# A first matrix product in 21 half-size products a step for 22, with one crossed tile of the convolution

## The chip, the cores and the metric

The kernel runs on one core of one Trainium2 chip. The metric is the device time in microseconds of one execution. The kernel before takes 2438.4 us, the median of three runs (2438.39 to 2438.45). The execution that the profile shows took 2438.89 us.

## The reference

The input `x` holds 8 sequences of 4096 tokens with 192 channels, in float32. A causal convolution of seven taps runs along the tokens; the taps are the softmax of an 8 x 7 weight, one row for each group of 24 channels. The result goes through a two-layer network with a gelu in between:

```python
w = softmax(weight, axis=-1)                       # 8 heads x 7 taps
y[b, s, c] = sum(w[c // 24, k] * x_pad[b, s + k, c] for k in range(7))
h = y.reshape(32768, 192) @ w_in                   # 192 x 2048
g = h / (1 + exp(-1.702 * h))
out = g @ w_out                                    # 2048 x 192
```

`w_in` and `w_out` arrive in float64 and are rounded to float32 inside the kernel. All matrix products are in float32.

## The kernel before

The work goes in 64 steps of 512 tokens (two halves of T = 256 tokens from two halves of the batch). Two neighbouring steps, an even and an odd one, share one "big" block of convolved input, so there are 32 big blocks.

A step has two matrix products on TensorE. The first, `product1` (L374 to L386), multiplies a block of `w_in` (64 channels by 256 columns) with a block of the convolved input (64 channels by 256 tokens). A call issues four matmuls, each of which the profile shows as two records; the two row halves of the array work at the same time on different columns of `w_in`. The second, `product2` and `quarters` (L470 to L500), multiplies 32-column pieces of `w_out` with the gelu's output `g`, four pieces at a time in the four column groups of the array.

Both products use sums of blocks to need fewer block products, in the manner of Strassen and Winograd. The first product has two units of work a step, one for each half of the columns of `w_in`. A unit is a product of 2 by 3 by 2 blocks (column halves, channel blocks of 64, token halves), which takes 12 block products plainly and 11 here, so a step has 22. The class `Unit` (L388 to L468) names them: `p1` to `p7` write into the PSUM tiles `slots` and `sums`, `seed` copies a partial product from a slot to `sums`, `keep2` and `keep3` copy intermediate results out, `add22` and `add12` add them on VectorE, and `h11` to `h22` apply the gelu on ScalarE. `sum_g` (L464) forms the four sums of `g` that the second product needs. Step 0 uses the plain form, 24 block products.

The convolved input is in the tile `f`. Its 128 partitions hold the 64 channels of the even step's tokens in the lower half and those of the odd step's tokens in the upper half. As both row halves of the array need the tokens of the step in hand, a copy of each half in the other half is made by `cross` (L351), two DMAs on SP's queue (SyncE). In the kernel before, `f` has room for both: index 0 of its second axis is the original and index 1 the crossed copy, and the pool holds two such tiles.

The order of instructions on each engine is the order in which they are written (`manual_schedule`). The preparation of the next big block is a list of pieces, `prepare` (L360 to L372): transposes of `x`, the load of the block after it, 21 convolution operations, four sums of `f` (`sums_c`) and the crossing. `work(n)` takes the next n pieces and issues them at that place. In an odd step one call `work(None)` (L732), in the middle of the first product, takes all that is left. `output` (L532 to L572) holds the second product, the final adds and transposes (`Out.turn`), and the six stores (`Out.store`, on SP's queue).

Within `output`, the last product p7 is followed on VectorE by two adds, a transpose, a subtraction and a transpose (L567 to L571), and the stores wait for these transposes. The main loop (L698 to L766) ends with `output`, and the next step's first `product1` follows it directly on TensorE.

Of the kernel before, what the change touches and what calls it, by code (L numbers as in the profile page):

```python
# [15 lines left out]
def kernel(  # L16
# [7 lines left out]
):  # L24

# [24 lines left out]
    P = 128  # L50
# [28 lines left out]
    hu_pool = ctx.enter_context(tc.tile_pool(name="hu", bufs=2))  # L79
# [42 lines left out]
    NB = 9  # L122
    C11, C12, C21, C22, C31, C32, V1, V2, V4 = range(NB)
    V3 = C12


    NA = 10
    W11, W12, W13, W21, W22, W23, X1, X2, X4, X5 = range(NA)
    X3 = W21
    w_in_s = consts.tile([P, NU, NA, UW], F32)  # L130
# [14 lines left out]
    assert PIECE == CW * D and NW * 2 * PIECE == 3 * NK * T and 6 * PIECE == 2 * NB * T  # L145
    raw = g[:, T1 : T4 + 1, :, :].rearrange("p s f t -> p (s f t)").bitcast(U32)
    raw = raw.rearrange("p (i n) -> p i n", i=NW)
    diag = consts.tile([P, NC, K, P], F32)
    assert min(NC * K * P, 2 * NJ * XW) >= 3 * PIECE

    def scratch(flat):
        return [flat[:, j * PIECE : (j + 1) * PIECE].bitcast(U32) for j in range(3)]

    tmp = f_pool.tile([P, 2, NB, T], F32, name="f").rearrange("p o b t -> p (o b t)")
    sets = [
        scratch(tmp),
        scratch(tmp[:, 3 * PIECE :]),
        None,
        scratch(diag.rearrange("p c k q -> p (c k q)")),
# [87 lines left out]
    def round_w_in(i):  # L247
        u, m = divmod(i, 2)
        dst = w_in_s[:, u, NC * m : NC * (m + 1), :]
        round_piece(i, [(lambda v: v.rearrange("p (k f) -> p k f", k=NC), dst)])  # L250

    def sums_w_in(u):
        a = [w_in_s[:, u, i, :] for i in range(NA)]
        vec.tensor_add(a[X1], a[W21], a[W22])
        vec.tensor_sub(a[X3], a[W11], a[W21])
        vec.tensor_sub(a[X2], a[X1], a[W11])
        vec.tensor_sub(a[X4], a[W12], a[X2])
        vec.tensor_sub(a[X5], a[W13], a[W23])
# [43 lines left out]

    for h in range(2):
        for j in range(2):
            nc.tensor.matmul(
                sums[:, h, j * T : j * T + P],
                ident,
                ident,
                start=(j == 0),
                stop=False,  # L310
                skip_group_check=True,
            )
            nc.tensor.matmul(
                sums[:, h, j * T + P : (j + 1) * T],
                ident,
                ident,
                start=False,
                stop=True,
                skip_group_check=True,
            )  # L320

# [13 lines left out]
    def conv(big, c, k):  # L335
        src = conv_src(big, c, k)
        dst = fs[big][:, 0, 2 * c : 2 * c + 2, :]
        tap = cw[:, c, k : k + 1]
        if k == 0:
            vec.tensor_scalar_mul(dst, src, tap)  # L340
        else:
            vec.scalar_tensor_tensor(  # L342
                out=dst, in0=src, scalar=tap, in1=dst, op0=ALU.mult, op1=ALU.add
            )

    def sums_c(big, i):
        f = [fs[big][:, 0, j, :] for j in range(NB)]
        dst, a, b = [(V1, C12, C11), (V3, C22, C12), (V2, C22, V1), (V4, C21, V2)][i]
        vec.tensor_sub(f[dst], f[a], f[b])  # L349

    def cross(big, b0=0, b1=NB, queue=nc.sync):  # L351

        f = fs[big]
        for o in range(2):
            queue.dma_start(out=f[halves[1 - o], 1, b0:b1, :], in_=f[halves[o], 0, b0:b1, :])

    def new_f(big):
        fs[big] = f_pool.tile([P, 2, NB, T], F32, name="f")

    def prepare(big):  # L360

        for c in range(NC):
            yield lambda c=c: transpose_x(big, c)
        if big + 1 < N_BIG:
            yield lambda: load_x(big + 1)
        yield lambda: new_f(big)
        for c in range(NC):
            for k in range(K):
                yield lambda c=c, k=k: conv(big, c, k)
        for i in range(4):  # L370
            yield lambda i=i: sums_c(big, i)
        yield lambda: cross(big)  # L372

    def product1(slot, a, b, s, u, first=False):  # L374
        f, o = fs[s // 2], s % 2
        for j in range(2):
            for h in range(2):
# [3 lines left out]
                    w_in_s[halves[h], u, a, j * P : (j + 1) * P],  # L381
                    f[halves[h], 0 if h == o else 1, b, :],
# [5 lines left out]
    class Unit:  # L388


        def __init__(self, s, u):
            self.s, self.u = s, u
            n = NU * s + u
            self.x, self.z = slots[n % 3], slots[(n - 1) % 3]
            self.u2 = self.u3 = None

        def pe(self, slot, a, b, first=False):
            product1(slot, a, b, self.s, self.u, first)

        def gelu(self, b, src):  # L400
            j = NK // NU * self.u
            act.activation(  # L402
                g[:, b, j : j + NK // NU, :].rearrange("p f t -> p (f t)"),
                src.rearrange("p h n -> p (h n)"),
                AF.Gelu_apprx_sigmoid,
            )

        def p1(self):
            self.pe(self.x, W11, C11, True)

        def seed(self):
            act.copy(sums, self.x)  # L412

        def p6(self):
            self.pe(sums, X2, V2)

        def keep2(self):
            self.u2 = hu_pool.tile([P, 2, TOK], F32, name="u2")
            act.copy(self.u2, sums)  # L419

        def p5(self):
            self.pe(self.z, X1, V1, True)

        def p5b(self):
            self.pe(self.z, W23, C32)

        def p7(self):
            self.pe(sums, X3, V3)

        def keep3(self):  # L430
            self.u3 = hu_pool.tile([P, 2, TOK], F32, name="u3")
            act.copy(self.u3, sums)  # L432

        def p2(self):
            self.pe(self.x, W12, C21)
            self.pe(self.x, W13, C31)

        def h11(self):
            self.gelu(B11, self.x)

        def p4(self):
            self.pe(sums, W22, V4)
            self.pe(sums, W23, C31)

        def h21(self):
            self.gelu(B21, sums)

        def add22(self):
            vec.tensor_add(self.u3, self.u3, self.z)  # L449

        def h22(self):
            self.gelu(B22, self.u3)

        def p3(self):
            self.pe(self.z, X4, C22)
            self.pe(self.z, X5, C32)

        def add12(self):
            vec.tensor_add(self.u2, self.u2, self.z)  # L459

        def h12(self):
            self.gelu(B12, self.u2)

        def sum_g(self, i):  # L464
            j = NK // NU * self.u
            v = [g[:, b, j : j + NK // NU, :] for b in range(NS)]
            dst, a, b = [(T1, B12, B11), (T2, B22, T1), (T3, B22, B12), (T4, T2, B21)][i]
            vec.tensor_sub(v[dst], v[a], v[b])  # L468
# [63 lines left out]
    def output(s, last, work):  # L532

        ra, rb = last.x, last.z
# [8 lines left out]
        for i in range(4):  # L543
            last.sum_g(i)
        p2, p3c = product2(rb, 0, (A12, B21), (S4, B22, 1))
        act.copy(chunk(p3, 1), p3c)  # L546
        work(2)
        vec.tensor_add(u2, u1, p2)
        out.turn(0, 0, u2)
        work(2)  # L550
# [3 lines left out]
        work(3)  # L554
# [9 lines left out]
        work(3)  # L564
# [11 lines left out]
    def work(n=None):  # L576
# [121 lines left out]
    for s in range(1, N_ST):  # L698
# [28 lines left out]
        if s > 2:  # L727
            b.p1()
# [68 lines left out]
```

## Time and profile before

| | us |
|---|---|
| median of the runs | 2438.4 |
| profiled execution | 2438.89 |
| its span, first to last instruction | 2437.2 |
| TensorE matmuls busy | 2423.5 (99%) |
| VectorE busy | 1837.7 (75%) |
| ScalarE busy | 1064.9 (44%) |
| first product, matmuls into the slots and into sums | 845.3 and 512.4 |
| second product, matmuls L476 | 1133.3 |

Busy time is the time in which an engine had at least one instruction of the kind; the sums of the groups overlap. A group is written as line, engine, operation, output<-inputs, shapes and count, then busy time in total and the mean length of one in ns, then the engine's idle time just before these instructions and what ended it. A timeline gives start and length in us, and joins equal neighbours. "SPq" is the issue of DMAs on SyncE's queue.

### The profile page before, as it was taken

What the parts mean: (1) busy time and instruction counts of PE and PEld (TensorE: products, weight loads), DVE (VectorE), ACT (ScalarE), POOL (GpSimd) and SP (SyncE); (2) the same over time, 40 slices, a digit from 0 to 9 for tenths busy, and PEclk for the clock granted to TensorE, in tenths of its full rate; (3) what the DMA queues carried; (4) which work ended last, traced back from release to release, by engine and by line L of the source; (5) the groups of instructions that cost most, each with busy time, mean ns of one, the idle gap of its engine ahead of it and who ended that gap; (6) DMA issues with size and microseconds to landing.
All of it is one profiled execution on the core that took longest, in us unless ns stands there. A gap on an engine that the chain in (4) does not pass through costs nothing.

```text
span 2437.2 us, 71539 instructions
## 1 busy us (share of the span) xinstructions
PE 2423.5 (99%) x32882; PEld 1786.0 (73%) x32882; DVE 1837.7 (75%) x2600; ACT 1064.9 (44%) x1370; POOL 7.5 (0%) x27
## 2 busy tenths in 40 slices
PE   9999999999999999999999999999999999999998
PEld 6767777777777777777777777777777777777776
DVE  8777777777877778777777777787777777777755
ACT  5435344444453444444534444445344344353443
POOL 1000000000000000000000000000000000000000
PEclk9999999999999999999999999999999999999999
DMA  7321222212122121222122221212212122212010
GB/s 179 76 51 35 46 45 58 51 34 58 33 58 58 37 49 35 57 57 52 34 49 42 58 54 32 58 33 57 59 39 47 37 55 58 52 34 52 14 34 15
DMA packets 191421, 120.81 MB, mean 50 GB/s; under 512 B 109904, under 2 KB 185296, under 8 KB 187152
## 3 DMA queue, kind: packets, MB, share of 16 engines
q1 hardware_dynamic: 190272, 115.32, 22.5%
q8 instruction: 257, 4.21, 0.7%
q0 software_dynamic: 288, 0.79, 0.1%
q14 instruction: 44, 0.36, 0.1%
q10 hardware_dynamic: 560, 0.13, 0.0%
HBM read 53.15 MB, written 25.17 MB: 32 GB/s over the span
## 4 chain that ended last, share of the span: by engine, by line
PE 97%; DVE 2%; DMA 1%; ACT 0%; issue 0%; SPq 0%; ACTq 0%
PE slot L476 45%; PE slot L379 31%; PE sums L379 18%; PE slot L492 2%; DVE f L342 1%; DMA f<-f 0%; DMA xin<-in_x_dram 0%; DVE u L449 0%; DVE osb L510 0%; SPq L103 0%; ACT g L402 0%; DVE g L468 0%; DVE xt L325 0%; ACT u L419 0%; DVE f L349 0%
## 5 line engine op out<-in xcount | busy, mean ns | idle before, releaser
L476 PE MATMUL slot<-g,w_out_s 128*32 128x256 f32 x20544 | 1133.3, 379 | 0.0
L476 PEld LDWEIGHTS slot<-g,w_out_s 128*32 128x32 f32 x20544 | 661.1, 110 | 451.0 <-issue 21.2
L379 PE MATMUL slot<-f,w_in_s 64*128 64x256 f32 x7200 | 845.3, 376 | 1.9 <-DVE u L449 0.9
L468 DVE TENSOR_TENSOR g<-g 128x1024 f32<-128x1024 f32 x504 | 599.9, 1221 | 214.5 <-ACT g L402 210.1
L379 PEld LDWEIGHTS slot<-f,w_in_s 64*128 64x128 f32 x7200 | 693.5, 187 | 90.6 <-DVE u L449 2.7
L379 PE MATMUL sums<-f,w_in_s 64*128 64x256 f32 x4080 | 512.4, 379 | 1.1 <-ACT u L432 1.1
L379 PEld LDWEIGHTS sums<-f,w_in_s 64*128 64x128 f32 x4080 | 390.9, 187 | 70.1 <-issue 25.1
L342 DVE SCALAR_TENSOR_TENSOR f<-xt,cw,f 128x512 f32<-128x512 f32 x564 | 421.4, 747 | 14.1
L402 ACT ACTIVATE g<-u 128x1024 f32<-128x1024 f32 x252 | 266.2, 1056 | 13.7 <-DVE u L459 13.6
L402 ACT ACTIVATE g<-sums 128x1024 f32<-128x1024 f32 x128 | 131.0, 1024 | 245.5 <-PE sums L379 245.5
L459 DVE TENSOR_TENSOR u<-u,slot 128x1024 f32<-128x1024 f32 x126 | 153.2, 1216 | 111.5 <-PE slot L379 111.4
L419 ACT COPY u<-sums 128x1024 f32<-128x1024 f32 x126 | 127.5, 1012 | 133.2 <-PE sums L379 133.2
L449 DVE TENSOR_TENSOR u<-u,slot 128x1024 f32<-128x1024 f32 x126 | 153.1, 1215 | 35.3 <-PE slot L379 32.9
L402 ACT ACTIVATE g<-slot 128x1024 f32<-128x1024 f32 x132 | 135.4, 1027 | 46.3 <-PE slot L379 46.3
L432 ACT COPY u<-sums 128x1024 f32<-128x1024 f32 x126 | 127.2, 1010 | 35.7 <-PE sums L379 35.7
L558 DVE TENSOR_TENSOR u<-u,slot 96x256 f32<-96x256 f32 x63 | 26.3, 418 | 143.2 <-ACT u L557 143.2
L557 ACT COPY u<-slot 32x256 f32<-32x256 f32 x63 | 23.1, 367 | 249.0 <-PE slot L492 249.0
L412 ACT COPY sums<-slot 128x1024 f32<-128x1024 f32 x126 | 126.8, 1006 | 2.9 <-PE slot L379 0.7
L510 DVE STREAM_TRANSPOSE osb<-u 96x256 f32<-96x256 f32 x253 | 111.2, 439 | 6.9 <-ACT u L690 0.4
L552 ACT COPY u<-slot 32x256 f32<-32x256 f32 x63 | 23.0, 365 | 194.4 <-PE slot L476 194.4
L546 ACT COPY u<-slot 32x256 f32<-32x256 f32 x63 | 23.1, 367 | 170.5 <-PE slot L476 170.5
L566 ACT COPY u<-slot 32x256 f32<-32x256 f32 x63 | 23.1, 366 | 141.1 <-PE slot L476 141.1
(87 smaller groups left out, 677.7 us busy)
## 6 DMA issues: line engine op xcount, KB each, us to landing
xin<-in_x_dram SPq DMA_DIRECT2D x240, 180.0 KB, 4.3
f<-f SPq DMA_DIRECT2D x62, 576.0 KB, 4.7
out_dram<-osb SPq DMA_DIRECT2D x382, 64.0 KB, 1.8
g<-in_moe_w_in_dram SPq DMA_DIRECT2D x8, 384.0 KB, 9.3
g<-in_moe_w_out_dram SPq DMA_DIRECT2D x4, 768.0 KB, 5.3
xin<-in_x_dram SPq DMA_DIRECT2D x16, 160.0 KB, 3.4
f<-f POOLq DMA_DIRECT2D x6, 128.0 KB, 5.5
f<-f SPq DMA_DIRECT2D x2, 192.0 KB, 2.8
```

The costliest lines, as they stand in the source:

```text
L342: vec.scalar_tensor_tensor(out=dst, in0=src, scalar=tap, in1=dst, op0=ALU.mult, op1=ALU.add)
L379: nc.tensor.matmul(slot[:, h, j * T : (j + 1) * T], w_in_s[halves[h], u, a, j * P : (j + 1) * P], f[halves[h], 0 if h == o else 1, b, :], ...
L402: act.activation(g[:, b, j : j + NK // NU, :].rearrange("p f t -> p (f t)"), src.rearrange("p h n -> p (h n)"), AF.Gelu_apprx_sigmoid,)
L412: act.copy(sums, self.x)
L419: act.copy(self.u2, sums)
L432: act.copy(self.u3, sums)
L449: vec.tensor_add(self.u3, self.u3, self.z)
L459: vec.tensor_add(self.u2, self.u2, self.z)
L468: vec.tensor_sub(v[dst], v[a], v[b])
L476: nc.tensor.matmul(dst[l * Q : (l + 1) * Q, :], w_out_s[:, a, j, c * Q : (c + 1) * Q], g[:, b, j, :], start=(first and j == 0), stop=(j == ...
L492: nc.tensor.matmul(dst[l], w_out_s[:, a, j, c * Q : (c + 1) * Q], g[:, b, j, :], start=(i == 0), stop=(i == NK // 4 - 1), skip_group_check ...
L510: vec.transpose(self.osb[:, n, :, m * Q : (m + 1) * Q], src.rearrange("p (j t) -> p j t", t=Q),)
```

## The change

The first product is no longer two units of 2 by 3 by 2 blocks but one product of 4 by 3 by 2 blocks (four quarters of the columns of `w_in`, three channel blocks, two token halves), which takes 24 block products plainly and 21 here (`TERMS`). The sums of blocks of `w_in` that these use (`SUMS_W`, 20 operations) are formed once, during steps 0 and 1; the sums of blocks of `f` (`SUMS_C`, eight operations instead of four) once for each big block. The new function `hidden` writes out the order of a step's 21 products, six copies on ScalarE, six operations on VectorE and eight gelus. Step 1 takes the plain form (24 products, `second_step`). One product of the next step, term 16, is issued ahead at the end of `hidden` (`fetch`), and its result copied to `sums` (`begin`).

The crossed copy moves out of `f` into a tile of its own, `crossed`, of which there is one; `f` keeps two buffers of the original alone. `cross` now sends one half at a time. For the even step it is sent in three parts: the block V1, which term 16 reads, as soon as it is formed, and the other blocks (four before V1, eight after it) at the end of `prepare`. For the odd step it is sent whole after the odd step before it has ended (832 KB).

`prepare` convolves the channel blocks in the order 0, 2, 1, forms V1 after the first two, and has 37 pieces. A step takes them in portions of 2, 2, 3 and 1 in `hidden` and 4 and 2 in `output`; `need(label)` takes pieces until the one with the label has gone. `work(None)` is gone. Eight matmuls on the identity at the start are removed, the scratch space of the rounding of the weights is laid elsewhere, and the sums of `g` are formed at other places of the same step. The core of the diff:

```diff
-    NB = 9
-    C11, C12, C21, C22, C31, C32, V1, V2, V4 = range(NB)
-    V3 = C12
+    NB = 13
+    C11, C12, C21, C22, C31, C32, V2, V3, V4, V5, V6, V7, V8 = range(NB)
+    V1 = C31
+    crossed = consts.tile([P, NB, T], F32)
+    SUMS_C = [
+        (V1, C31, "-", C11), (V2, V1, "-", C32), (V3, C12, "+", V2), (V4, C22, "+", V2),
+        (V5, C21, "-", V4), (V6, C11, "-", V5), (V7, C22, "-", C21), (V8, C32, "-", C22),
+    ]
...
+    TERMS = [
+        (14, V2), (10, C21), (20, V5), (6, V3), (19, V6), (0, C11), (17, C32), (5, V8), (4, V7), (8, V1), (12, C22),
+        (9, C12), (13, V4), (3, V3), (15, C22), (16, V6), (2, V1), (1, C21), (11, C11), (7, V7), (18, C12),
+    ]
...
-    def cross(big, b0=0, b1=NB, queue=nc.sync):
-        f = fs[big]
-        for o in range(2):
-            queue.dma_start(out=f[halves[1 - o], 1, b0:b1, :], in_=f[halves[o], 0, b0:b1, :])
+    def cross(big, o, b0=0, b1=NB, queue=nc.sync):
+        queue.dma_start(
+            out=crossed[halves[1 - o], b0:b1, :], in_=fs[big][halves[o], b0:b1, :]
+        )
...
     def prepare(big):
         for c in range(NC):
-            yield lambda c=c: transpose_x(big, c)
+            yield "", lambda c=c: transpose_x(big, c)
         if big + 1 < N_BIG:
-            yield lambda: load_x(big + 1)
-        yield lambda: new_f(big)
-        for c in range(NC):
+            yield "", lambda: load_x(big + 1)
+        yield "", lambda: new_f(big)
+        for c in (0, 2):
             for k in range(K):
-                yield lambda c=c, k=k: conv(big, c, k)
-        for i in range(4):
-            yield lambda i=i: sums_c(big, i)
-        yield lambda: cross(big)
+                yield "", lambda c=c, k=k: conv(big, c, k)
+        yield "", lambda: sums_c(big, 0)
+        yield f"first {big}", lambda: cross(big, 0, V1, V1 + 1)
+        for k in range(K):
+            yield "", lambda k=k: conv(big, 1, k)
+        for i in range(1, len(SUMS_C)):
+            yield "", lambda i=i: sums_c(big, i)
+        yield "", lambda: cross(big, 0, 0, V1)
+        yield f"all {big}", lambda: cross(big, 0, V1 + 1, NB)
...
-                    w_in_s[halves[h], u, a, j * P : (j + 1) * P],
-                    f[halves[h], 0 if h == o else 1, b, :],
+                    w_in_s[halves[h], a, j * P : (j + 1) * P],
+                    (f if h == o else crossed)[halves[h], b, :],
...
+    def hidden(s, x, z, y, work, fetch):
+        k15, k16, k19, k18, k20 = kept
+        def pe(slot, *ts, first=False):
+            terms(s, slot, *ts, first=first)
+        pe(sums, 12)
+        act.copy(k15, sums)
+        pe(x, 5, 17)
+        gelu(B11, 0, x)
+        pe(z, 7, first=True)
+        pe(sums, 0)
+        act.copy(k16, sums)
+        work(2)
+        pe(y, 6, 14, first=True)
+        vec.tensor_sub(x, z, k15)
+        work(2)
+        pe(sums, 13)
+        act.copy(k19, sums)
+        pe(x, 2)
+        act.copy(k18, x)
+        pe(z, 11)
+        pe(sums, 20, 10)
+        vec.tensor_sub(k15, y, k19)
+        gelu(B12, 0, sums)
+        pe(x, 4)
+        act.copy(k20, x)
+        vec.tensor_sub(k19, z, k19)
+        work(3)
+        gelu(B22, 1, k19)
+        gelu(B22, 0, k15)
+        pe(y, 8)
+        pe(sums, 1, 9, first=True)
+        pe(y, 15)
+        sum_g(0, T1)
+        vec.tensor_add(k20, k20, sums)
+        vec.tensor_sub(k16, y, k16)
+        gelu(B11, 1, k20)
+        pe(x, 18)
+        gelu(B21, 1, x)
+        gelu(B21, 0, k16)
+        sum_g(0, T2)
+        fetch()
+        pe(sums, 3, 19)
+        work(1)
+        vec.tensor_add(k18, k18, sums)
+        gelu(B12, 1, k18)
...
-    def output(s, last, work):
+    def output(s, ra, rb, work, between=None):
...
-        for i in range(4):
-            last.sum_g(i)
+        sum_g(1, T1)
+        sum_g(1, T2)
+        sum_g(1, T4)
+        sum_g(0, T4)
         p2, p3c = product2(rb, 0, (A12, B21), (S4, B22, 1))
         act.copy(chunk(p3, 1), p3c)
-        work(2)
         vec.tensor_add(u2, u1, p2)
         out.turn(0, 0, u2)
-        work(2)
+        sum_g(0, T3)
+        sum_g(1, T3)
...
-        work(3)
+        work(4)
+        if between:
+            between()
...
-        work(3)
+        work(2)
         p7, p4c = product2(ra, 0, (S3, T3), (A22, T4, 1))
...
+    def need(label):
+        while any(item[0] == label for item in todo):
+            work(1)
...
+    def fetch(s, slot):
+        need(f"first {s // 2}")
+        terms(s, slot, 16, first=True)
+    def begin(slot):
+        act.copy(sums, slot)
...
+    second_step(fetch_2)
+    for s in range(2, N_ST):
+        more = s + 1 < N_ST
+        hidden(s, x, z, y, work, lambda: fetch(s + 1, z) if more else None)
+        if more:
+            begin(z)
+        output(s, y, x, work)
+        if s % 2 and more:
+            need(f"all {(s + 1) // 2}")
+            cross((s + 1) // 2, 1)
+            todo.extend(prepare((s + 3) // 2) if (s + 3) // 2 < N_BIG else ())
+        x, z = z, x
```

## The prediction, made before the changed kernel was run

> **What bounds the kernel now.** The chain of work that ended last comes first, because it says which engine sets the time.
>
> ```profile
> PE 97%; DVE 2%; DMA 1%; ACT 0%; issue 0%; SPq 0%; ACTq 0%
> ```
>
> TensorE is the chain. The groups of instructions (count, then total busy time and mean ns, then idle time before them) show that hardly anything makes its matmuls wait: 1.9 and 1.1 us in the first product.
>
> ```profile
> L379 PE MATMUL slot<-f,w_in_s 64*128 64x256 f32 x7200 | 845.3, 376 | 1.9 <-DVE u L449 0.9 <-DMA f<-f 0.4 <-DVE u L568 0.3
> L379 PE MATMUL sums<-f,w_in_s 64*128 64x256 f32 x4080 | 512.4, 379 | 1.1 <-ACT u L432 1.1
> L349 DVE TENSOR_TENSOR f<-f 128x256 f32<-128x256 f32 x128 | 50.0, 409 | 1.1
> ```
>
> The timeline of TensorE over one step prices the rest (start us, length, instruction, records).
>
> ```profile
> 1239.56 3.62 PE L379 MATMUL slot<-f,w_in_s 64*128 64x256 f32 x32
> 1243.01 1.03 PE L379 MATMUL sums<-f,w_in_s 64*128 64x256 f32 x8
> ...
> 1251.74 14.02 PE L476 MATMUL slot<-g,w_out_s 128*32 128x256 f32 x256
> 1265.58 1.05 PE L492 MATMUL slot<-g,w_out_s 128*32 128x256 f32 x16
> 1266.44 3.64 PE L476 MATMUL slot<-g,w_out_s 128*32 128x256 f32 x64
> 1270.01 1.13 PE L379 MATMUL sums<-f,w_in_s 64*128 64x256 f32 x8
> ```
>
> One product is 8 records. Four take 1243.01 - 1239.56 = 3.45 us, so a product costs **0.863 us**. The second product runs from 1251.74 to 1270.01, 18.27 us. Steps repeat every 37.46 us (starts of the x256 runs, 1214.28 and 1251.74). At 1270.01 step 32 ends and step 33 begins at once. What happens at such a seam decides this case, so I read VectorE and then SP's queue across it.
>
> ```profile
> 1268.47 1.32 DVE L563 TENSOR_TENSOR u<-u,slot 32x256 f32<-32x256 f32 x3
> 1269.82 1.54 DVE L342 SCALAR_TENSOR_TENSOR f<-xt,cw,f 128x512 f32<-128x512 f32 x2
> 1271.28 0.42 DVE L349 TENSOR_TENSOR f<-f 128x256 f32<-128x256 f32 x1
> 1271.73 0.42 DVE L567 TENSOR_TENSOR u<-u,slot 96x256 f32<-96x256 f32 x1
> 1272.07 0.41 DVE L568 TENSOR_TENSOR u<-u,slot 96x256 f32<-96x256 f32 x1
> 1272.40 0.43 DVE L510 STREAM_TRANSPOSE osb<-u 96x256 f32<-96x256 f32 x1
> 1272.76 0.38 DVE L570 TENSOR_TENSOR u<-u,u 96x256 f32<-96x256 f32 x1
> 1273.17 0.44 DVE L510 STREAM_TRANSPOSE osb<-u 96x256 f32<-96x256 f32 x1
> 1273.54 1.17 DVE L349 TENSOR_TENSOR f<-f 128x256 f32<-128x256 f32 x3
> ```
>
> ```profile
> 1272.86 2.83 SPq L525 DMA_DIRECT2D out_dram<-osb  x6
> 1275.80 1.11 SPq L355 DMA_DIRECT2D f<-f  x2
> ```
>
> Here the last sums of the convolution (L349) come after the seam, and the crossing transfers queue behind six stores. But this is the seam from an even to an odd step, and the block is first read by `nxt.p1`, behind 16 of the odd step's products: 13.8 us after the seam, at 1283.8. The two transfers of another such pair land 4.7 and 7.5 us after issue (issues 467 to 595 ns each), so the later one at about 1276.3 + 7.5 = 1283.8, just in time:
>
> ```profile
> L355 SPq DMA_DIRECT2D f<-f x2: 467/531/595, 1425.7 to 1426.2; - x2
> ...
> DMA to landing us min/median/max: 4.7/6.1/7.5
> ```
>
> [...]the 128-column start matmuls at L305 and L313 start about 0.43 us apart for two records (8.34, 8.77, 9.19), while the 512-column L587 matmuls after 10.08 take 0.43 us each, half the time per column. [...]p7 was done at 1270.01, yet L567 stands until 1271.73 behind convolution work. [...]
>
> **The change, part by part.**
>
> *Products.* Before: 24 in step 0 and 63 x 22 = 1410 (11280 records / 8, as the groups count). After: 24 in step 0, 24 in step 1, 62 x 21 = 1350. Step 1 gains two, each later step loses one. **-60 x 0.863 = -51.8 us.** A later step is then 37.46 - 0.863 = 36.6 us.
>
> *Copies and adds inside a step.* ScalarE: six copies and eight activations as before. VectorE: six 128x1024 operations on partial products instead of four (+2 x 1.22 us), eight sums of g as before, eight sums of f per pair of steps for four (+0.8 us a step). VectorE goes from 1837.7/64 = 28.7 to about 32 us of a 36.6 us step. I walked the new step by hand, with 0.26 us from a product's end to the copy that reads it (1233.52 to 1233.78 in the trace), 1.01 for copies, 1.03 to 1.06 for activations, 1.22 for VectorE. The 21 products end at 18.1 us; the tightest waits are sums for k16 (copied at 5.6, wanted at 6.0), for k19 (8.2 against 8.6) and for B12 (11.65 against 12.1); x for x - z (5.8 against 6.9). All are met with 0.4 us or more. Cost nothing; without that cover some 0.4 us each. In the second product S1, S2 and S3 meet T1, T2, T3 1.7 us or more early.
>
> *The early crossing.* V1 alone (64 KB) is sent in the odd step, at about 11.8 us, lands 2.5 us later (the 64 KB pair of the old kernel), and is wanted by the fetched product at 15.5. Hidden, by 1 us.
>
> *The late crossing, at every seam from an odd to an even step.* `prepare` now has 37 pieces, and a step takes 2+2+3+1+4+2 = 14. After two steps nine are left: seven sums of f (V2 to V8) and the two transfers to `crossed`. They are forced out by `need("all ...")` after `output`, behind the last transposes; the order of VectorE's instructions in the changed kernel shows exactly that. The first product of the next step is term 12, which reads V4 from `crossed`, and TensorE waits there for the second transfer. `crossed` is single, but its other readers are a step away; what is late is the data. From the end of p7, t, with the prices of the seam shown:
>
> - two convolution pieces before the last adds: L563 ended at t - 0.22, + 1.53 = t + 1.3;
> - two adds and a transpose: 1272.83 - 1271.73 = 1.1, so turn(1,1) at t + 2.4; the second transpose lets the sums start 0.7 later, at t + 3.1;
> - seven sums at 0.39 (1.17 for three): **t + 5.9**;
> - SP: six stores from t + 2.4, 2.9 us to the next issue: t + 5.3; the 256 KB transfer's issue 0.55: t + 5.9; both paths meet, and the 512 KB transfer is issued at **t + 5.95**;
> - landing: 4.7 us for 576 KB in the pair above, less 0.3 for 64 KB less, plus up to 0.8 for the 256 KB just ahead: 4.4 to 5.2, I take 4.95: **t + 10.9**.
>
> The old kernel gives this transfer 13.8 us after a seam; the new one gives it none. So TensorE stands 10.9 us. Behind term 12 waits its whole queue, the copies of ScalarE with it. On VectorE two transposes of the next block come after the sums, and on SP the 832 KB transfer for the odd step, not wanted for 36 us, and then a load of x; all of that lies inside the stall or has a step's time. Pairs of tokens 2 to 31 have such a seam (pair 1 is prepared within the plain step): **30 x 10.9 = +327 us.** Bounds: 9.6 (a landing in 3.6) and 13.4 (in 7.5, if the 832 KB transfer issued next shares the engines).
>
> *Restart at half clock.* The trace of before can't price it. [...] I take 2.2[...]: **30 x 2.2 = +66 us.**
>
> *Start and step 1.* Eight identity matmuls go; L587 may then begin at half clock, 0 to +2 us. Steps 1 to 3 hold some 4 us more than the later ones (39.45 between runs for 37.46); part may go. Together 0, within 3.
>
> Sum against the profiled execution: 2438.9 - 51.8 + 327 + 66 = **2780 us** (the median of the runs is 0.5 less than that execution).
>
> **Rivals.**
>
> *The stall is as said, the clock stays up* (12 in 100): 2438.9 - 51.8 + 327 = 2714.
>
> *The transfers share* (12 in 100): landing in 7.5, stall 13.4: 30 x 15.6 = 468, so 2855.
>
> *The step itself waits* (13 in 100): VectorE at 32 of 36.6 us and margins of 0.4 us break; two of 0.4 in each of 62 steps, +50: 2830.
>
> *Faster: the seam is hidden* (3 in 100): the sums' transfer is there when p7 ends, and only the products count: 2387. It decides below 51.8/30 = 1.7 us a seam. Against it: even a transfer that took nothing leaves t + 5.9.
>
> **How the numbers follow.** The forecast itself has 60 in 100; its own range, 30 x (11.9 to 14.4), is 2745 to 2820. The range 2700 to 2855 takes in the first two rivals' centres and the third, and leaves the faster case and double mishaps out. A difference under 0.2% can't be told from none. Faster 0.03; within 0.2%, with a seam near 1.7 us, 0.01; slower 0.96.
>
> **What would show it.** Matmuls of the first product fall to 10800 records. They wait for the crossing DMA about 30 times, some 325 us in all, none before about 180 us; TensorE's share of the chain falls to about 88%, with VectorE, SP and DMA in the rest. The x256 runs keep 14.0 us. After a seam the first 4 to 5 us of products take 1.7 us each. I am wrong if those waits are short, or if odd steps wait as well.

## The result, and the profile after

| | before | after |
|---|---|---|
| median of the runs, us | 2438.4 (2438.4 to 2439.3) | 2782.4 (2781.4 to 2784.0) |
| profiled execution, us | 2438.9 | 2784.0 |
| mean granted TensorE clock | 0.999 | 0.938 |

The ratio is 1.141, with a 95% interval of 1.139 to 1.143: the changed kernel is slower by 344 us. Line numbers from here on are those of the kernel named.

First the chain of work that ended last, of the changed kernel: by engine, then by line.

```profile
PE 83%; DMA 7%; DVE 7%; SPq 1%; issue 1%; ACT 0%; DVEq 0%
PE slot L502 36%; PE slot L414 25%; PE sums L414 19%; DMA crossed<-f 5%; PE slot L518 2%; DMA out_dram<-osb 2%; DVE f L374 2%; DVE u L592 1%; DVE osb L536 1%; DVE f L301 1%; SPq L551 1%; PE slot L620 1%; DVE u L589 0%; DVE u L596 0%; DVE u L587 0%
```

TensorE had 97% of the chain before. The transfer that fills `crossed` has come in, with VectorE behind it. The groups of TensorE's matmuls (busy us in total, mean ns of one, then idle us just before them and what ended it) say where:

```profile
L502 PE MATMUL slot<-g,w_out_s 128*32 128x256 f32 x20544 | 1133.5, 379 | 0.0
...
L414 PE MATMUL slot<-f,w_in_s 64*128 64x256 f32 x3120 | 780.5, 396 | 0.2 <-DVE slot L463 0.2
L414 PE MATMUL slot<-crossed,w_in_s 64*128 64x256 f32 x3120 | 753.5, 391 | 0.0
L414 PE MATMUL sums<-crossed,w_in_s 64*128 64x256 f32 x2280 | 587.2, 393 | 171.5 <-DMA crossed<-f 171.5
L414 PE MATMUL sums<-f,w_in_s 64*128 64x256 f32 x2280 | 595.0, 393 | 129.3 <-DVE f L299 129.3
```

The first product has 3120 + 3120 + 2280 + 2280 = 10800 records, for 11280 before: the 60 products are gone. Its mean matmul is 391 to 396 ns, where before it was 376 to 379; the windows below show that some of them ran at a lower clock. The second product keeps its 379. In the first product TensorE waits 0.2 us in the whole run ahead of matmuls into `slot`, and 300.8 us ahead of those into `sums`. The view of waits (engine, line and what it waited for: us in total, times, longest) counts these:

```profile
PE sums L414 <- DMA crossed<-f: 171.5, 30, 7.4
PE sums L414 <- DVE f L299: 129.3, 30, 4.3
```

Thirty times each: once for every pair of steps from the third on. The first wait to end is that for a sum: half of the first product's matmuls read V4 from `f` itself, and two of these run before the queue stands again for V4 in `crossed`. One such seam, from an odd to an even step, in the timelines of TensorE, VectorE and SP's queue (start us, length, instruction, records, in brackets the idle time before it and what ended it):

```profile
1215.73 3.64 PE L502 MATMUL slot<-g,w_out_s 128*32 128x256 f32 x64
1223.71 0.79 PE L414 MATMUL sums<-f,w_in_s 64*128 64x256 f32 x2 [4.34 <-DVE f L299]
1230.37 0.79 PE L414 MATMUL sums<-crossed,w_in_s 64*128 64x256 f32 x1 [5.87 <-DMA crossed<-f]
...
1231.39 0.63 PE L414 MATMUL sums<-crossed,w_in_s 64*128 64x256 f32 x1
...
1231.82 0.63 PE L414 MATMUL sums<-crossed,w_in_s 64*128 64x256 f32 x1
```

```profile
1219.10 1.54 DVE L374 SCALAR_TENSOR_TENSOR f<-xt,cw,f 128x512 f32<-128x512 f32 x2
1220.67 0.42 DVE L596 TENSOR_TENSOR u<-u,slot 96x256 f32<-96x256 f32 x1
...
1221.34 0.43 DVE L536 STREAM_TRANSPOSE osb<-u 96x256 f32<-96x256 f32 x1
...
1222.48 0.38 DVE L301 TENSOR_TENSOR f<-f 128x256 f32<-128x256 f32 x1
1222.90 0.76 DVE L299 TENSOR_TENSOR f<-f 128x256 f32<-128x256 f32 x2
1223.69 1.55 DVE L301 TENSOR_TENSOR f<-f 128x256 f32<-128x256 f32 x4
```

```profile
1221.80 2.84 SPq L551 DMA_DIRECT2D out_dram<-osb  x6
1224.74 1.76 SPq L382 DMA_DIRECT2D crossed<-f  x3
```

p7 ends at t = 1219.30 (the first line's end, less the 0.07 us by which the next matmul overlaps it in the kernel before). With t for that moment, the adds begin at t + 1.4 and the sums at t + 3.2; the last sum ends at 1225.24, t + 5.9. The stores leave the queue to the crossing at t + 5.4, the second of the three transfers (512 KB) is issued at t + 6.0, and the product that needs it begins at t + 11.07. This stretch is called the stand below, though two matmuls run in it. Over the 30 seams its median is the same 11.07 us. The DMA issues give the landing (KB each, median us from issue to landing):

```profile
crossed<-f SPq DMA_DIRECT2D x31, 832.0 KB, 8.4
...
crossed<-f SPq DMA_DIRECT2D x31, 512.0 KB, 5.0
crossed<-f SPq DMA_DIRECT2D x31, 256.0 KB, 2.9
```

Then comes the slow restart: the matmuls of the crossed half follow each other every 0.43 us (1230.96 to 1231.39), where those after 1235 do so every 0.21 us (1235.27 to 1235.48). The view of windows (stretch in us, its length, busy us and records of TensorE, its weight loads, VectorE, ScalarE and GpSimd, then the granted TensorE clock, DMA share and GB/s) shows the clock:

```profile
1230.00:1231.00 1.00, 0.63 (x4) 0.54 (x6) 0.00 (x0) 0.00 (x0) 0.00 (x0) 0.50 1.04 226
...
1233.00:1234.00 1.00, 1.00 (x8) 0.73 (x7) 0.00 (x0) 0.55 (x1) 0.00 (x0) 0.50 0.08 16
1234.00:1235.00 1.00, 1.00 (x10) 0.86 (x8) 0.00 (x0) 0.00 (x0) 0.00 (x0) 0.79 0.00 0
1235.00:1236.00 1.00, 1.00 (x13) 0.87 (x12) 0.00 (x0) 0.75 (x1) 0.00 (x0) 1.00 0.00 0
```

It is 0.50 for four microseconds of matmuls and 1.00 again by 1235. It had fallen during the stand: it is 1.00 from 1223 to 1224 and 0.50 from 1225 to 1226.

The starts of the long runs of the second product add this up. From an even step to the odd one after it they are 36.60 us apart, but for the first (41.78), the last (35.73) and two others (36.78 and 37.04). From an odd step to the even one, from step 3 on, they are 49.0 to 52.1 us apart, 49.9 in the mean, so a seam costs 13.3 us: 11.07 of standing and some 2.2 of restart. The ledger is 30 x 13.3 - 51.8 = 347, against 345.1 between the two profiled executions.

### The profile page after: what moved, and what is told of

The parts are those of the page before. It is cut to its first block, busy times and chain, and to the rows that moved or that the text cites. A ratio compares the mean times of both kernels' runs of the same rounds, so it can differ in the third digit from the quotient of the medians.

```text
span 2782.2 us, 71248 instructions
## 1 busy us (share of the span) xinstructions
PE 2466.0 (89%) x32386; PEld 1836.1 (66%) x32386; DVE 2043.1 (73%) x2850; ACT 1054.3 (38%) x1364; POOL 7.5 (0%) x27
## 4 chain that ended last, share of the span: by engine, by line
PE 83%; DMA 7%; DVE 7%; SPq 1%; issue 1%; ACT 0%; DVEq 0%
PE slot L502 36%; PE slot L414 25%; PE sums L414 19%; DMA crossed<-f 5%; PE slot L518 2%; DMA out_dram<-osb 2%; DVE f L374 2%; DVE u L592 1%; DVE osb L536 1%; DVE f L301 1%; SPq L551 1%; PE slot L620 1%; DVE u L589 0%; DVE u L596 0%; DVE u L587 0%
## 5 line engine op out<-in xcount | busy, mean ns | idle before, releaser
L502 PEld LDWEIGHTS slot<-g,w_out_s 128*32 128x32 f32 x20544 | 661.0, 110 | 451.2 <-issue 11.9
L414 PE MATMUL slot<-crossed,w_in_s 64*128 64x256 f32 x3120 | 753.5, 391 | 0.0
L414 PE MATMUL sums<-crossed,w_in_s 64*128 64x256 f32 x2280 | 587.2, 393 | 171.5 <-DMA crossed<-f 171.5
L414 PE MATMUL sums<-f,w_in_s 64*128 64x256 f32 x2280 | 595.0, 393 | 129.3 <-DVE f L299 129.3
L414 PEld LDWEIGHTS slot<-crossed,w_in_s 64*128 64x128 f32 x3120 | 606.5, 197 | 61.4 <-issue 0.4
L414 PEld LDWEIGHTS sums<-crossed,w_in_s 64*128 64x128 f32 x2280 | 436.2, 194 | 235.3 <-DMA crossed<-f 189.8
L430 ACT ACTIVATE g<-kept 128x1024 f32<-128x1024 f32 x310 | 320.9, 1058 | 142.2 <-DVE kept L493 82.9
L463 DVE TENSOR_TENSOR slot<-slot,kept 128x1024 f32<-128x1024 f32 x62 | 76.2, 1229 | 301.4 <-ACT g L430 193.9
L455 ACT COPY kept<-sums 128x1024 f32<-128x1024 f32 x62 | 62.7, 1012 | 407.0 <-PE sums L414 407.0
L471 DVE TENSOR_TENSOR kept<-slot,kept 128x1024 f32<-128x1024 f32 x62 | 75.9, 1225 | 114.7 <-ACT kept L466 114.7
L483 DVE TENSOR_TENSOR kept<-kept,sums 128x1024 f32<-128x1024 f32 x62 | 75.7, 1221 | 67.9 <-PE sums L414 66.3
L466 ACT COPY kept<-sums 128x1024 f32<-128x1024 f32 x62 | 62.7, 1012 | 97.8 <-PE sums L414 97.8
```

Source lines behind the costliest of these rows:

```text
L414: nc.tensor.matmul(slot[:, h, j * T : (j + 1) * T], w_in_s[halves[h], a, j * P : (j + 1) * P], (f if h == o else crossed)[halves[h], b, :] ...
L430: act.activation(g[:, b, j : j + NK // 2, :].rearrange("p f t -> p (f t)"), src.rearrange("p h n -> p (h n)"), AF.Gelu_apprx_sigmoid,)
L455: act.copy(k15, sums)
L463: vec.tensor_sub(x, z, k15)
L466: act.copy(k19, sums)
L471: vec.tensor_sub(k15, y, k19)
```

## The experiments

Theory: at each of the 30 seams TensorE stands from p7's end until the late transfer has landed, and then runs at half clock for a while; the products themselves got cheaper by 51.8 us. Rivals: the 21 products wait inside the step, the single `crossed` tile makes someone wait, the transfers slow one another, or the products after a seam are slow for another reason than the clock. Each run below carries one edit of the changed kernel, unless it says otherwise.

### The preparation taken earlier

The pieces of `prepare` are taken in larger portions (the first tuple for even steps, the second for odd ones; the first four numbers in `hidden`, the last two in `output`), so that all sums of `f` and both transfers are issued before the odd step ends, and the 256 KB transfer is moved ahead of the sums. No product, copy or transfer is added or removed.

```diff
+        yield "", lambda: cross(big, 0, 0, V1)
         for i in range(1, len(SUMS_C)):
             yield "", lambda i=i: sums_c(big, i)
-        yield "", lambda: cross(big, 0, 0, V1)
         yield f"all {big}", lambda: cross(big, 0, V1 + 1, NB)
...
+    PORTIONS = ((2, 4, 4, 2, 5, 3), (2, 4, 4, 3, 4, 0))
     def hidden(s, x, z, y, work, fetch):
+        n = PORTIONS[s % 2]
...
-        work(2)
+        work(n[0])
...
-        work(2)
+        work(n[1])
...
-        work(3)
+        work(n[2])
...
-        work(1)
+        work(n[3])
...
+        n = PORTIONS[s % 2] if s > 1 else (0, 0, 0, 0, 4, 2)
         out = Out(s)
...
-        work(4)
+        work(n[4])
...
-        work(2)
+        work(n[5])
```

> All 37 pieces of the preparation are taken before the last product of the odd step (20 in the even step, 17 in the odd one), with the 256 KB transfer ahead of the sums. The theory (the whole loss is the late crossing and the restart it causes): the 512 KB transfer is issued some 5.5 us before the seam and is there when TensorE arrives, so the seams go and only the saved products count: 2438.4 - 51.8 + about 2 for the start = 2388 us, 2384 to 2396. Rival (the fuller VectorE makes the steps themselves wait, or the new form is slower in itself): steps longer than 36.6 us also away from the seams, above 2400 us.

Measured: **2384.0 us** (2383.8 to 2384.7), at the lower edge of the range expected; a ratio to the kernel before of 0.978, interval 0.976 to 0.979. This version beats both kernels. Its chain, and the same kind of seam in TensorE's timeline:

```profile
PE 99%; DVE 0%; DMA 0%; SPq 0%; issue 0%; ACT 0%; DVEq 0%
```

```profile
1348.40 3.64 PE L505 MATMUL slot<-g,w_out_s 128*32 128x256 f32 x64
1351.97 0.48 PE L414 MATMUL sums<-f,w_in_s 64*128 64x256 f32 x1
1351.97 0.48 PE L414 MATMUL sums<-crossed,w_in_s 64*128 64x256 f32 x1
```

The product on `crossed` begins 0.07 us before the end of p7's line, with no bracket: no wait. The mean clock is 1.000, and from step 2 on the steps repeat every 36.60 us, but for one of 36.73 and the last, 36.02. This shows the whole loss of 398 us (2782.4 - 2384.0) to be the lateness of the preparation. What is left is a gain of 54 us over the kernel before: 51.8 from the 60 products, the rest from the start and the first steps, taken apart below. VectorE is busy for 85% of the span and still TensorE waits for it nowhere after the start, so the rival of waits inside the step falls. So does the one of the single tile: `crossed` is as single here as before.

Against this version, a seam of the changed kernel costs 398.4 / 30 = 13.28 us. The same subtraction is used for the runs below.

### The start as well

The version above, with the eight identity matmuls of the kernel before put back at the start.

```diff
     vec.tensor_copy(cw, pw)
+    for h in range(2):
+        for j in range(2):
+            nc.tensor.matmul(
+                sums[:, h, j * T : j * T + P], ident, ident,
+                start=(j == 0), stop=False, skip_group_check=True,
+            )
+            nc.tensor.matmul(
+                sums[:, h, j * T + P : (j + 1) * T], ident, ident,
+                start=False, stop=True, skip_group_check=True,
+            )
```

> As the run with the pieces taken early, with the eight identity matmuls of the old start put back. The theory: the start's 28 matmuls of the convolution (14.9 us in the changed kernel, 12.5 before) are at full pace again, and the time falls by 1.8 us against the run without them. Rival (the start is set by the rounding of the weights): no difference, within 0.5 us.

Measured: 2383.2 us (2383.2 to 2383.4), 0.8 us less, between the two expectations. The 28 convolution matmuls at the start took 12.6 us instead of 14.6, as expected; but the second product of step 0 began at 44.81 instead of 45.76, so half of the 2 us was lost again in the start; TensorE now waits 0.32 us there for a crossing, and didn't without these matmuls. It is the best of all versions here, a ratio of 0.977 (0.976 to 0.979) to the kernel before.

### TensorE kept busy at the seam

To part the standing from the restart, TensorE is given useless matmuls at the seam. They write a PSUM bank (a part of the memory for matmul results) that is overwritten later; the transfer comes no earlier.

```diff
         if s % 2 and more:
+            for i in range(22):
+                nc.tensor.matmul(
+                    y[:, 1, T : 2 * T], w_in_s[:, 0, 0:P], fs[s // 2][:, C11, :],
+                    start=(i == 0), stop=(i == 21), skip_group_check=True,
+                )
             need(f"all {(s + 1) // 2}")
```

> The changed kernel with 22 matmuls of no use (128 x 128 by 256, results overwritten) at each of the 30 seams, 9.5 us of TensorE work inside the wait of 11.1 us. The theory (part of the loss is the array's restart at half clock after the wait): the wait ends at the same time, but the products after it run at full pace, 30 x 2.2 = 66 us less: 2716 us, 2700 to 2730. Rival (the wait alone is the loss): 2782 us or more.

Measured: 2746.7 us (2745.4 to 2749.3), about half way between theory and rival. The reason is the probe itself: its bank is read by the last adds of p7, so it waited 2.2 us for them at each seam and ended at t + 11.9, 0.9 us after the data had come. Its mean clock was 0.997, and the products after it went at full pace, their matmuls 0.21 us apart (1903.04 to 1903.25). A second run has 18 of these matmuls instead of 22.

> Eighteen useless matmuls at each seam instead of 22: begun 2.2 us after p7's end as in the run with 22, at 0.44 us each, they end at t + 10.1, about 0.9 us before the transfer lands, so they no longer hold the products back and still keep TensorE from standing long. Theory (what the changed kernel loses at a seam is the wait of 11.07 us and, beyond it, only the half clock after it): seams repeat after 36.60 + 11.07 = 47.7 us, the products after a seam run at full pace, total 2438.9 - 51.8 + 30 x 11.07 - 2 = 2717, between 2710 and 2724. Rival (the first products after a seam are slowed by something else, such as the transfers still moving): it stays above 2740.

Measured: 2735.7 us (2732.8 to 2736.7), outside the 2710 to 2724 expected, but 47 us below the changed kernel. Two seams in TensorE's timeline, and two windows of each in the clock:

```profile
1625.90 8.01 PE L767 MATMUL slot<-f,w_in_s 128*128 128x256 f32 x36 [2.19 <-DVE u L597]
...
1879.48 9.70 PE L767 MATMUL slot<-f,w_in_s 128*128 128x256 f32 x36 [2.19 <-DVE u L597]
```

```profile
1621.15:1624.56 3.41, 2.56 (x48) 1.30 (x40) 3.20 (x7) 0.73 (x2) 0.00 (x0) 1.00 0.02 5
1624.56:1627.98 3.42, 2.08 (x10) 1.87 (x11) 3.32 (x9) 0.00 (x0) 0.00 (x0) 1.00 0.18 39
...
1877.15:1880.56 3.41, 1.22 (x9) 1.00 (x6) 3.31 (x8) 0.37 (x1) 0.00 (x0) 1.00 0.00 0
1880.56:1883.98 3.42, 3.42 (x10) 2.71 (x9) 3.32 (x9) 0.00 (x0) 0.00 (x0) 0.50 0.61 133
```

In 12 of the 30 seams the useless matmuls take 8.0 us; where nothing else is late, their steps repeat after 47.7 us, 36.60 + 11.07, as the theory said. In the other 18 they take 9.7 us, because the granted clock is 0.50 for 3.41 us (from 1880.56 to 1883.98 in the seam shown). The pause of 2.19 us ahead of them is the same in both. The windows shown are cut in steps of 3.413 us from the fall of the clock at 1880.56 (1624.56 lies 75 steps before it): in the seam that is slowed the whole pause falls into one window (busy 1.22 of 3.41 us), in the other it is split between two (2.56 and 2.08). That this is what decides is my reading of these two seams. At the slowed seams the useless matmuls end 0.8 us after the data, and the step repeats after 48.5. So 18 x 0.8 = 15 us of the 19 us above 2717 are explained by the probe. The products after a seam run at full pace in both cases (at 1889.43 and 1889.64 in the slowed seam, 0.21 us apart, with the clock at 1.00), although the same transfers are moving (213 GB/s from 1889 to 1890): what slows the products after a seam of the changed kernel is the clock.

### Sums ahead of the last adds

`need` is called before the two last adds of the odd step instead of after the transposes, so the seven sums go ahead of these on VectorE and the transfers ahead of the six stores on SP's queue.

```diff
         act.copy(chunk(p4, 1), p4c)
+        if s % 2 and s > 1:
+            need(f"all {(s + 1) // 2}")
         vec.tensor_add(u1, u1, p7)
```

> The changed kernel with the nine remaining pieces (seven sums, two transfers) issued before the last adds and transposes of the odd step's output, so that neither the transposes nor the six stores stand before them. The theory (VectorE's and SP's in-order queues each cost the crossing about 2 us): sums done at 4.05 us after the seam for 5.9, the 512 KB transfer issued at once, landing at 8.5 for 11.0; 30 x 2.5 = 75 us less: 2707 us, 2695 to 2722. Rival (the transfer itself is the whole wait, whenever it is issued): within 15 us of 2782.

Measured: 2695.8 us (2694.9 to 2696.4), at the lower edge of the range expected. The stand is 8.27 us in the median, and the two waits show both halves of it shorter:

```profile
PE sums L414 <- DMA crossed<-f: 151.7, 30, 5.2
PE sums L414 <- DVE f L299: 72.7, 30, 2.5
```

The sums end at t + 4.05 instead of t + 5.9, and the 512 KB land in 4.1 us instead of 5.0. Two things have changed for them: the 256 KB, which need no sum, are now issued at t + 1.4 and land at t + 4.2, as the 512 KB are issued, and the 832 KB are issued at t + 9.4, after the stores, when the 512 KB have landed. This run doesn't part the two.

### Two transfers on ScalarE's queue

The 256 and the 512 KB transfers are issued on ScalarE's queue instead of SP's, for all blocks after the second.

```diff
-        yield "", lambda: cross(big, 0, 0, V1)
-        yield f"all {big}", lambda: cross(big, 0, V1 + 1, NB)
+        yield "", lambda: cross(big, 0, 0, V1, act if big > 1 else nc.sync)
+        yield f"all {big}", lambda: cross(big, 0, V1 + 1, NB, act if big > 1 else nc.sync)
```

> The changed kernel with the two late transfers of the even step issued on ScalarE's queue instead of SP's. The sums still end 5.9 us after the seam, so getting past the stores gains nothing. But the 832 KB transfer, until now behind the 512 KB one in one queue, is issued on SP at the same time. The theory[...]: the 512 KB lands 6 to 7 us after issue for 5.0, 30 x 1.5 = 45 us more: 2827 us, 2800 to 2850. Rival (the queues don't hinder each other): 0 to 0.6 us less a seam, 2765 to 2782. Second rival (SP's queue of stores is what delays the crossing): more than 1 us a seam less, below 2750.

Measured: 2751.2 us (2747.7 to 2752.6). My expectation was wrong: I thought that 832 KB on the other queue, issued in the same microsecond, would slow the 512 KB. The result lies between the ranges of the two rivals, too; a seam costs 1.04 us less. The DMA issues of this run:

```profile
crossed<-f SPq DMA_DIRECT2D x31, 832.0 KB, 8.3
crossed<-f ACTq DMA_DIRECT2D x30, 512.0 KB, 4.4
crossed<-f ACTq DMA_DIRECT2D x30, 256.0 KB, 2.8
```

The 512 KB land in 4.4 us, sooner than the 5.0 on one queue; the 832 KB take the delay. The stand is 10.38 us in the median, 0.7 less. The 512 KB are issued at t + 6.0 as before, since they wait for the sums, so the stores on SP's queue are not what held them. The 256 KB, which wait neither for sums nor for stores now, go out at t + 1.4 and have landed at t + 4.2. That they are no longer just ahead of the 512 KB would explain the shorter landing, but this is argued, not shown. The seam costs (2751.2 - 2384.0) / 30 = 12.24 us, so that the restart is 1.9 us here; most seams repeat after about 48.73 us, a value that the changed kernel never reaches. With the 36.60 of the other step that is 85.33 us, 25 times the 3.413 us of the windows above. At the seams at 875.47, 960.83 and 1046.15, which follow each other after 85.36 and 85.32 us, the matmuls ran at half pace for the same 3.57 us. That accounts for the 31 us gained: 30 x 0.7 from the stand and 30 x 0.35 from the restart.

### The block V4 first

The first product after the seam reads only V4 from `crossed`. It is summed among the first and sent alone (64 KB); the rest follows in three parts.

```diff
-        for i in range(1, len(SUMS_C)):
+        for i in range(1, 4):
             yield "", lambda i=i: sums_c(big, i)
+        yield "", lambda: cross(big, 0, V4, V4 + 1)
         yield "", lambda: cross(big, 0, 0, V1)
-        yield f"all {big}", lambda: cross(big, 0, V1 + 1, NB)
+        for i in range(4, len(SUMS_C)):
+            yield "", lambda i=i: sums_c(big, i)
+        yield "", lambda: cross(big, 0, V4 + 1, NB)
+        yield f"all {big}", lambda: cross(big, 0, V1 + 1, V4)
```

A first run had V2 in place of V1 + 1 in the last line: it leaves out the crossing of the block C32, 64 KB of the last part.

> The changed kernel with the late crossing cut into four and sent in the order of use: V4 (64 KB, all that the first product needs), the four blocks before V1 (256 KB), V5 to V8 (256 KB), V2 and V3 (128 KB). The theory (the landing of the 512 KB is 5 of the 11 us, and its size counts): V4 is issued at 5.35 after the seam and lands 2.5 to 3 later, TensorE starts at 8.3 for 11.1, and the rest arrives under the first three products; 30 x 2.6 = 78 us less: 2705 us, 2690 to 2730. Rival (a landing takes as long whatever its size, or four transfers hold each other up): 2770 us or more.

Measured: 2663.0 us (2660.2 to 2665.4). This is 42 us less than expected, and below the whole range: the seam costs 9.3 us, where 2705 would have been 10.7. I had taken 2.5 to 3 us for the landing of V4, and it took 1.9; the rest of the difference is a shorter restart. With C32 in place:

> V4 first again, now with the crossing of C32 included, in the last of the four parts (C32, V2, V3: 192 KB for 128 KB). Theory: the seam is set by V4's landing alone, t + 7.4 as in the run before, and the part that grew is wanted only after four more products: 2663, between 2655 and 2675. Rival: V2 and C32 now land after the products that read them are reached, another 0.3 to 1 us at each seam: 2672 to 2695.

Measured: 2662.7 us (2661.9 to 2664.7). The 64 KB more cost nothing, and no part after V4 is waited for. V4 is issued as soon as the stores have left SP's queue, lands in 1.9 us, and the stand is 7.35 us. TensorE's waits:

```profile
PE sums L418 <- DVE f L299: 129.3, 30, 4.3
PE sums L418 <- DMA crossed<-f: 57.0, 31, 3.1
```

The wait for the sums is that of the changed kernel to a tenth; only the wait for the transfer has shrunk, from 171.5.

### All seams together

| kernel | median, us | stand, us (median of its seams) | whole seam: (time - 2384.0) / 30 | rest |
|---|---|---|---|---|
| changed kernel | 2782.4 | 11.07 | 13.28 | 2.2 |
| two transfers on ScalarE's queue | 2751.2 | 10.38 | 12.24 | 1.9 |
| sums ahead of the last adds | 2695.8 | 8.27 | 10.39 | 2.1 |
| V4 first, complete | 2662.7 | 7.35 | 9.29 | 1.9 |
| 18 useless matmuls | 2735.7 | 11.07, filled | 11.72 | 0.7 |
| prepared earlier | 2384.0 | none | 0 | 0 |

The rest hardly depends on how long TensorE stood, between 7 and 11 us, and most of it goes when TensorE is kept busy. That is what a restart at half clock predicts, and what neither the transfers in flight nor the length of the wait would do. The clock in the traces gives the same loss directly: half of the time that it still stood at 0.50 after the data had come is 2.22, 1.89, 2.22 and 1.84 us in the mean of the 30 seams, in the order of the first four rows, and nothing in the last two.

## Why the prediction was right

The forecast was 2780, with 2745 to 2820 for its own case; 2782.4 was measured.

*Products, -51.8.* Right: 10800 records, and steps of 36.60 us wherever no seam comes in, as worked out from 37.46 - 0.863. The run prepared earlier gives the gain without the seams: -54.4, which is the 51.8 and what the start and the first steps add.

*Copies and adds inside a step, nothing.* Right. TensorE's waits inside the steps sum to 0.2 us, so the margins of 0.4 us were enough.

*The early crossing, nothing.* Right; the 64 KB land in 1.9 us, for the 2.5 taken.

*The late crossing, 10.9 a seam.* Right, term by term: adds at t + 1.3 (measured 1.4), sums from t + 3.1 (3.2) to t + 5.9 (5.9), the issue at t + 5.95 (6.0), landing 4.95 (5.0), together 10.9 (11.07). It is 5 us of 345 short. The landing was the one term with wide bounds, and the estimate hit it with some luck: 4.4 for the transfer and 0.55 for the 256 KB ahead of it, where a 512 KB transfer without close neighbours takes 4.1 (prepared earlier, or sums first) and the neighbours together add 0.9. With the 832 KB still beside it but the 256 KB long landed it took 4.4 (on ScalarE's queue), which points to the 256 KB for most of the 0.9. The upper bound of 7.5, with equal sharing between it and the 832 KB behind, did not come true on one queue or on two.

*Restart, 2.2 a seam.* Right in the mean, 2.22 by the clock of the trace, and the kind of cause is shown by the filled seams. The 2.2 was my estimate; no trace of the kernel before shows it. That it was right to the tenth is luck: single seams lost 1.5 to 3.1 us, and with other stands the mean went down to 1.84. Of two seams of the changed kernel, one had half clock for 3.2 us after 1057.13, the other for 5.9 us after 1143.23, so 1.6 and 2.9 us lost. A stand of 11 us is not needed to halve the clock: in the run with 18 useless matmuls it was halved after a pause of 2.2 us in 18 of 30 seams and not in the other 12.

*Start, within 3.* The matmuls of the convolution at the start took 14.9 us for 12.5, and the second product of step 0 began 1.8 us later than before (46.44 for 44.61). In return the 4 us that the first steps held above the later ones went: the starts of the second products of steps 0 to 3 are 41.78, 38.29 and 36.60 us apart, for 41.83, 39.45 and 39.44 before. That is 4.05 us less, though these three steps have as many products as before. With both, the ledger is 30 x 13.3 - 51.8 + 1.8 - 4.05 = 345.0, for 345.1 measured. 2.3 us of it are waits that TensorE had in these steps before (1.1, 0.9 and 0.3 us in the lines of the prediction), for 0.2 us after; for the rest the cause stays open.

*What would show it.* All held but two. After a seam of the changed kernel the matmuls of a product followed each other every 0.43 us, four times for a product of 1.7 us, for 4.4 us in the mean. The waits for the crossing DMA were to sum to some 325 us, and they sum to 171.5: another 129.3 us are waits for VectorE's sum V4. The prediction had overlooked that half of the first product's matmuls read V4 from `f`, where it is ready only at t + 4.4; the moment at which the crossed half can start, and so the cost, is the same. And TensorE's share of the chain was to fall to 88% and fell to 83%. I took the share to fall to what TensorE's waits leave of the span, 325 of 2780 us being 12%. But at a seam the chain runs back from the transfer over VectorE's sums, a store, and VectorE's adds and convolution pieces to 1215.98, before p7 has ended: it leaves TensorE for 14.4 us (1215.98 to 1230.37), not for 11.07. 30 x 14.4 is 15.5% of the span.

Of the rivals, the one with the clock kept up (2714) is refuted by the windows at 0.50; its size, 2714, is near what 18 useless matmuls would give if all seams were as the 12 good ones, 2717. Sharing transfers (2855) are refuted by landings of 5.0 and 4.4 us; waits inside the step (2830) by the 0.2 us. The hidden seam (2387) was wrong for this kernel, but its number is the time that the kernel has when it is true: 2384.0.

## What to carry to other kernels

When a change adds pieces to a list of work that is dealt out in portions, count them against the portions: here 37 against 28 left nine pieces, on no busy engine's account, for the one place where every engine waits for them. Price a stall by walking each queue from a fixed event to the landing of the data, and add what the restart of TensorE is measured to cost; in this kernel that was 1.84 to 2.22 us in the mean, for stalls of 7 to 11 us. A large loss from such a cause is no verdict on the idea beside it: dealing out the same pieces earlier turned 344 us lost into 54 us gained.

## What the runs showed of the hardware

- The granted clock that the profiler recorded for the changed kernel is 1.00 or 0.50. In its trace cut into windows of 3.413 us, with one edge at 1224.185, all 783 windows from 101.2 us on show one of the two values throughout: every change lies on an edge. At the 30 seams the half clock lasted 10.24 us (20 times) or 13.65 us (10 times), three or four windows.
- In the same windows of the same trace, by the profile's busy time of TensorE: the 30 windows at 1.00 that were followed by 0.50 were busy for 0 to 0.70 us of the 3.41, the 652 that were followed by 1.00 for 1.74 us or more. The 30 windows at 0.50 that were followed by 1.00 were busy for 3.00 us or more, the 70 that were followed by 0.50 for 2.77 us or less. In the run with 18 useless matmuls a window busy for 1.22 us was followed by 0.50, and two of 2.56 and 2.08 us by 1.00. The mean clock of that run was 0.988, with 22 of these matmuls 0.997, and without them 0.938.
- A restart after a stand of 7 to 11 us cost 1.4 to 3.1 us of TensorE's time in the four runs that have one, half of the 2.7 to 6.1 us for which matmuls were slowed after the data had come. In the changed kernel the clock came back 3.2 us after the data of 1057.13 and 5.9 us after those of 1143.23. With the stand shortened by 0.7 us, on ScalarE's queue, the mean was 1.89 us, and the three seams from 875.47 to 1046.15 lost 1.8 us each.
- Two transfers issued at the same time on different queues did not share evenly: 512 KB on ScalarE's queue landed in 4.4 us (4.1 in the version prepared earlier), 832 KB on SP's in 8.3 (5.9 there). Of the delay, 0.3 us fell on the smaller transfer and 2.4 us on the larger.
- Transfers from one half of the partitions to the other landed in 1.9 us (64 KB), 2.8 (256 KB), 4.1 (512 KB) and 5.9 (832 KB) in the version prepared earlier: about 1.55 us and 5.2 us a megabyte, an estimate fitted to these four.
